# A third weight's products split into even and odd banks in every second unit of a fused FFT and max-out kernel

## The chip, the cores and the metric

The kernel runs on one core of a Trainium2 chip. Its engines work from queues of their own and meet through semaphores: TensorE (PE in the profile; its weight loads are PEld), VectorE (DVE), ScalarE (ACT), GpSimd (POOL) and SyncE (SP, which here only issues DMAs). Matmuls write to PSUM, which has eight banks of 512 float32 per partition; GpSimd is given SBUF operands only in this kernel. The metric is the device time of one execution in microseconds.

## The reference

```python
# x: (8, 3072, 256)
X = np.fft.fft(x, axis=1)
X = np.fft.fft(X, axis=2)
t = X.real.astype(np.float32).reshape(8 * 3072, 256)
# w1, w2, w3: (256, 768), w_out: (768, 256)
h = np.maximum(np.maximum(t @ w1, t @ w2), t @ w3)
out = (h @ w_out).astype(np.float32)
```

So there is a real part of a two-dimensional Fourier transform for each of 8 batches, and then a feed-forward layer of 24,576 tokens whose hidden value is the maximum over three products.

## The kernel before, in words

**The mathematics.** For each batch the transform over the sequence is made in two stages, and the transform over the 256 features is not made at all: it is multiplied into the weights beforehand. A batch leaves two tables per feature, an even part `tE` and an odd part `tO`, each 128 partitions by 1536 positions. Position k and position 3072 - k use the same two tables: one needs "even plus odd", the other "even minus odd". The kernel calls them plus and minus, and the hidden values `hp` and `hm`. Partition 0 of `tO` is an exception: it holds a part that keeps its sign.

The maximum of three products is written as w1's product plus max(0, product with w2 - w1, product with w3 - w1). `gE[i]` and `gO[i]` hold the even and odd halves of the two difference weights (i = 0 for w2, i = 1 for w3), and `gD[i]` is `gO[i]` times `dif`, which is 0 on partition 0 and -2 elsewhere: adding `gD` times `tO` turns plus into minus. w1's own part goes straight through w_out as `gw`.

**The units.** The main loop (from L685) runs over 8 batches, 3 blocks of 512 positions in each, and 6 column groups `jc` of 128 hidden features: 18 units a batch, 144 in all. A unit has

- `unit_plus` (L392): four 512-column matmuls, gE and gO into the bank `pse2` and gE and gO into the bank `pse3`;
- `unit_out` (L409): ScalarE's relu of `pse2` into `stmp` (L412), then VectorE's maximum of `pse3` and `stmp` into `hp` (L413);
- `unit_minus` (L402): two matmuls with gD that add to the same two banks, and `unit_out` again into `hm`. These are issued in the next unit's turn, by `finish`, which is called behind that unit's plus.

Behind this, each unit issues ten steps of layer 2 (`l2_some(10)`), which work on the hidden values of the block before: `l2_block` (L426) makes, for each of four slots of 128 positions, one 512-column matmul (L445) and twelve 256-column ones (L422) into a bank `po`, and for two slots together two more (L437) that ScalarE copies to `even`. VectorE adds the two into `ot` (L450). SP stores the plus half (L462); GpSimd stores the minus half, whose rows run backwards, with an indirect DMA, the scatter (L455), and a small memset behind it (L459).

**The transform of the next batch** is spread over the units by a plan written out by hand (`at`, `piece`, `late`, `ahead0`, `ahead`): `s` pieces (L336) multiply x into `tb`, `y` stores that to DRAM, `z` loads it back transposed as `yb`, `x0` and `c` put in a separate row, which GpSimd copies into `yb` (L374), and `k` pieces (L376) make 512 positions of `tE` or `tO`, copied by ScalarE (L383). In inner batches the `s` pieces stand in units 1 to 4, `z` in 7, `c` in 11 and the `k` pieces in 13 to 17. `fetch` (L650) makes GpSimd load x of a batch, in four parts, into one of two buffers; `turn` (L654) makes VectorE write a mirrored copy of it (L126, L127). Both have places in the plan: for batch b, fetches in units 9 to 12 and mirrors in units 14 to 17 of batch b - 2.

**What sets the order.** Every engine executes in the order in which the Python program issues: there is no scheduler. Waits come from tile dependencies and from pools. PSUM is divided as `ps_f` 2 banks (transform pieces, `pl`, some products of the preparation), `ps_l1` 2 each for `pse2` and `pse3`, and `ps_o` 2 for `po`.

**The start.** Before the loop, x of batch 0 is loaded and mirrored, angles are computed by VectorE (L255), tables by ScalarE (L260), the first halves of the weights are multiplied by the feature transform (L274, L286), and the first `k` pieces are made: `m.k(0, 0, dve)` (L590), whose copy is VectorE's, and `m.k(1, 0)` (L591). `angles(1024, NHALF + 1)` stands ahead of them (L587).

## Time and profile before

| | us |
|---|---|
| median of 3 runs | 418.67 (417.16 to 418.86) |
| the profiled execution | 418.88 |
| its span | 417.1 |
| PE busy | 397.2 (95%) |
| DVE busy | 293.2 (70%) |
| ACT busy | 251.7 (60%) |
| POOL busy | 151.1 (36%) |
| one inner batch | 47.15 |

The page's second part cuts the span in 40 slices: PE shows 9 in nearly all slices behind the start, DVE mostly between 5 and 8, POOL mostly between 1 and 6. An inner batch is a stretch such as 217.74 to 264.90, from one batch's first `hm` to the next's. Matmul records last longer than the distance between them, because they are pipelined: for the time that a matmul costs, read the distance between starts. The same holds, to a smaller degree, for VectorE's operations.

### The profile page before, as it was taken

The numbers are of one execution on the slowest core, as the hardware profiler recorded it, in microseconds if no ns is written. First come the engines' busy times: TensorE is split into PE (matmuls) and PEld (weight loads), VectorE is DVE, ScalarE is ACT, GpSimd is POOL, SyncE is SP. The second block draws the span as 40 slices with busy tenths as digits, with TensorE's granted clock in tenths as the row PEclk, the third lists the DMA queues.
The fourth block names the chain that finished last, engine by engine and source line by source line (L and its number), as shares of the span: only waits on it lengthen the run. The fifth ranks groups of instructions, "written<-read, shape, count | busy, mean of one in ns | idle before, by whom it ended". The sixth has DMA issues, their size and how long they took to land.

```text
span 417.1 us, 8143 instructions
## 1 busy us (share of the span) xinstructions
PE 397.2 (95%) x2741; PEld 249.1 (60%) x2790; DVE 293.2 (70%) x524; ACT 251.7 (60%) x474; POOL 151.1 (36%) x269
## 2 busy tenths in 40 slices
PE   7669899999999999999999999999999999999995
PEld 2235456666666666666666666656665666656664
DVE  7868656867785677857785676857785676667772
ACT  2547667665666657675567657675567656655550
POOL 7370123423622443323632443324532432333430
PEclk9989999999999999999999999999999999999998
DMA  8998246936952579236962569235962552222224
GB/s 123 193 179 129 65 120 159 175 93 159 199 139 68 122 186 186 81 89 151 203 148 60 133 174 193 85 88 125 223 149 60 139 159 65 78 61 63 83 75 127
DMA packets 66334, 53.27 MB, mean 128 GB/s; under 512 B 34649, under 2 KB 61890, under 8 KB 65094
## 3 DMA queue, kind: packets, MB, share of 16 engines
q0 software_dynamic: 23376, 26.27, 32.3%
q1 hardware_dynamic: 41748, 25.82, 23.7%
q10 hardware_dynamic: 1168, 0.65, 0.6%
q8 instruction: 22, 0.36, 0.4%
q14 instruction: 20, 0.16, 0.1%
HBM read 35.14 MB, written 31.69 MB: 160 GB/s over the span
## 4 chain that ended last, share of the span: by engine, by line
PE 84%; DVE 6%; ACT 3%; DMA 3%; issue 2%; POOL 1%; DVEq 0%; SPq 0%; ACTq 0%; POOLq 0%
PE po L422 28%; PE pse L398 15%; PE pse L406 13%; PE pse L399 12%; PE po L445 4%; PE ps L340 4%; PE pl L437 3%; PE ps L381 2%; DMA xt<-in_x_dram 2%; DVE hm L413 2%; ACT stmp L412 2%; DVE xt L126 1%; POOL xt L121 1%; DMA out_dram<-ot 1%; DVE ot L450 0%
## 5 line engine op out<-in xcount | busy, mean ns | idle before, releaser
L412 ACT ACTIVATE stmp<-pse 128x512 bf16<-128x512 f32 x288 | 169.9, 601 | 81.7 <-PE pse L399 61.0
L455 POOL DMA_INDIRECT out_dram<-ot,rows_m x92 | 103.8, 1128 | 238.4 <-DVE ot L450 209.4
L413 DVE TENSOR_TENSOR hp<-pse,stmp 128x512 bf16<-128x512 f32 x144 | 99.6, 691 | 105.0 <-PE pse L406 63.8
L398 PE MATMUL pse<-tE,gE 128*128 128x512 bf16 x287 | 109.4, 381 | 4.5 <-DVE tE L383 2.7
L413 DVE TENSOR_TENSOR hm<-pse,stmp 128x512 bf16<-128x512 f32 x144 | 99.0, 688 | 1.0 <-ACT stmp L412 0.9
L399 PE MATMUL pse<-tO,gO 128*128 128x512 bf16 x249 | 95.0, 382 | 0.1
L422 PE MATMUL po<-wout_bf,hp 128*128 128x256 bf16 x576 | 86.1, 273 | 0.0
L406 PE MATMUL pse<-tO,gD 128*128 128x512 bf16 x280 | 83.9, 379 | 0.5
L422 PE MATMUL po<-wout_bf,hm 128*128 128x256 bf16 x576 | 78.6, 273 | 0.0
L422 PEld LDWEIGHTS <-hp 128*128 128x128 bf16 x576 | 56.4, 98 | 26.1
L422 PEld LDWEIGHTS <-hm 128*128 128x128 bf16 x576 | 56.4, 98 | 16.3
L450 DVE TENSOR_TENSOR ot<-po,even 128x512 f32<-128x512 f32 x92 | 62.9, 683 | 0.2
L406 PEld LDWEIGHTS <-gD 128*128 128x128 bf16 x288 | 27.6, 98 | 32.0
L342 ACT CAST tb<-ps 128x512 bf16<-128x512 f32 x48 | 26.1, 588 | 28.4 <-PE ps L340 27.2
L399 PEld LDWEIGHTS <-gO 128*128 128x128 bf16 x288 | 28.2, 98 | 25.0 <-issue 4.1
L398 PEld LDWEIGHTS <-gE 128*128 128x128 bf16 x288 | 28.3, 98 | 22.5 <-issue 1.0
L445 PE MATMUL po<-gw,tO 128*128 128x512 bf16 x92 | 34.9, 379 | 0.0
L340 PE MATMUL ps<-xt,tabz 128*128 128x512 bf16 x96 | 25.1, 379 | 4.5 <-DVE xt L127 4.4
L441 ACT COPY even<-pl 128x512 f32<-128x512 f32 x46 | 27.0, 587 | 0.0
L383 ACT CAST tO<-ps 128x512 bf16<-128x512 f32 x24 | 14.1, 586 | 16.9 <-PE ps L381 9.3
L121 POOL DMA_DIRECT2D xt<-in_x_dram x36 | 23.4, 657 | 0.0
L126 DVE COPY xt<-xt 64x1524 bf16<-64x1524 bf16 (+4 forms) x32 | 19.1, 598 | 5.1 <-DMA xt<-in_x_dram 4.4
(134 smaller groups left out, 219.4 us busy)
## 6 DMA issues: line engine op xcount, KB each, us to landing
yb<-db SPq DMA_DIRECT2D x7, 833.0 KB
xt<-in_x_dram POOLq DMA_DIRECT2D x14, 384.0 KB
out_dram<-ot SPq DMA_DIRECT2D x56, 96.0 KB
out_dram<-ot SPq DMA_DIRECT2D x64, 64.0 KB
db<-tb SPq DMA_DIRECT2D x21, 192.0 KB
xt<-in_x_dram POOLq DMA_DIRECT2D x7, 400.0 KB
xt<-in_x_dram POOLq DMA_DIRECT2D x7, 368.0 KB
out_dram<-ot SPq DMA_DIRECT2D x64, 32.0 KB
```

Source lines behind the costliest of these rows:

```text
L121: return nc.gpsimd.dma_start(out=xt[b % 2][32 * h:32 * h + 32, lo:hi, :], in_=src)
L340: nc.tensor.matmul(ps1, tab_at[hh], self.x[:, 8 * k + hh:8 * k + 8:2, 0:128], start=(hh == 0), stop=(hh == 1))
L398: nc.tensor.matmul(pse[:, 0:n], gE[i][:, js], te, start=True, stop=False)
L399: nc.tensor.matmul(pse[:, 0:n], gO[i][:, js], to, start=False, stop=True)
L406: nc.tensor.matmul(pse, gD[i][:, js], to, start=False, stop=True, skip_group_check=True)
L412: nc.scalar.activation(out=stmp[:, 0:n], in_=pses[0][:, 0:n], func=AX.Relu)
L413: nc.vector.tensor_tensor(out=dst, in0=src3, in1=stmp[:, 0:n], op=ALU.max)
L422: nc.tensor.matmul(po, hcols(jc), wout_bf[:, jc * 256:(jc + 1) * 256], start=False, stop=(jc == NJC - 1), skip_group_check=True)
L441: nc.scalar.copy(out=even, in_=pl)
L445: nc.tensor.matmul(po, to[:, cp], gw[:, 256:768], start=True, stop=True)
L450: nc.vector.tensor_tensor(out=ot.rearrange("p (h c) -> p h c", h=2), in0=po.rearrange("p (h c) -> p h c", h=2), in1=lin.unsqueeze(1).to_br ...
L455: stored(nc.gpsimd.indirect_dma_start(out, bass.IndirectOffsetOnAxis(ap=rows_m[0:128 - lo, b * 12 + slot: b * 12 + slot + 1], axis=0), ot[ ...
```

## The change

From unit 7 of the whole run on, every odd unit is *split*. A split unit's third weight no longer goes through plus and minus in one bank. Instead `third(g)` makes the even product gE[1] times tE into one bank `e3` and gD[1] times tO into another, `d3`. ScalarE copies `d3` times -0.5, which is the odd part without its partition 0. VectorE copies `e3` and adds partition 0's part: the row `tO[0]`, spread to all partitions in `vb`, times a column of weights `wcol`. GpSimd adds and subtracts the two copies into `plus3` and `minus3`. The unit's own output is then one VectorE operation: the maximum of 0, `pse2` and `plus3`, and for minus the same with `minus3`. ScalarE has no relu in split units.

`third(g)` is issued in the turn of unit g - 2, behind the minus of unit g - 3 (for units 7 and 13, in the turn before their own). The row `tO[0]` is written to DRAM (`vds`) by SP and read back with a broadcast (`v`), both in the plan near the `k` pieces, whose order in `late` is changed. The column `wcol` is made once, in unit 5, with 24 one-column matmuls.

Other moves come with it. PSUM is divided anew: `ps_f` 3, `pse2` 2, one bank for `pse3` of even units (`ps_w3`), `ps_o` 2. The scatter is issued in the unit after its slot. A batch's minus of its last unit is carried into the next batch. x is fetched a batch earlier, in units 9 to 12 of batch b - 3, and mirrored in units 5, 7, 9 and 11 of batch b - 2. In the start, the tables for 512 to 1024 follow the second product, the last angles go to units 6 and 7 and their tables to units 8 and 9, and two warm-up matmuls are dropped. The middle positions' steps (`l2_mid`) are made in two goes.

```diff
-    ps_f = ctx.enter_context(tc.tile_pool(name="ps_f", bufs=2, space=bass.MemoryType.PSUM))
+    ps_f = ctx.enter_context(tc.tile_pool(name="ps_f", bufs=3, space=bass.MemoryType.PSUM))
...
+    def angle(part, c0=1024, c1=NHALF + 1):
+        cs = slice(c0, c1)
+        if part == 0:
+            scal(kvec[:, cs], kvec[:, cs], s_of, ALU.mult, phi, ALU.add)
+            scal(q[:, cs], kvec[:, cs], 1.0 / 3072.0, ALU.mult, ROUND, ALU.add)
+        else:
+            scal(q[:, cs], q[:, cs], -ROUND, ALU.add, -3072.0, ALU.mult)
+            nc.vector.tensor_tensor(out=kvec[:, cs], in0=kvec[:, cs], in1=q[:, cs], op=ALU.add)
...
+    def column():
+        psc = ps_f.tile([128, 512], FP32, name="psc", tag="ps")
+        for jc in range(NJC):
+            for k, (table, wt) in enumerate(((md, w3_bf), (nmd, w1_bf))):
+                for fc in range(2):
+                    nc.tensor.matmul(psc[:, jc:jc + 1],
+                                     wt[:, fc * DFF + jc * 128: fc * DFF + jc * 128 + 128],
+                                     table[fc][:, 128:129],
+                                     start=(k == 0 and fc == 0), stop=(k == 1 and fc == 1))
+        nc.scalar.copy(out=wcol, in_=psc[:, 0:NJC])
...
             evict(out=(self.tE, self.tO)[which][:, g * 512:(g + 1) * 512], in_=ps2)
+            if which and (self.b or g):
+                cs = slice(g * 512, (g + 1) * 512)
+                nc.sync.dma_start(out=vds[self.b % 2][:, cs], in_=self.tO[0:1, cs])
+
+        def v(self, g):
+            cs = slice(g * 512, (g + 1) * 512)
+            nc.sync.dma_start(out=self.vb[:, cs],
+                              in_=vds[self.b % 2][:, cs].to_broadcast([128, 512]))
...
-            stored(nc.gpsimd.indirect_dma_start(
...
-            nc.gpsimd.memset(mark, 0.0)
+            waiting.append((b * 12 + slot, lo, ot))
...
-    tables(512, 1024)
     for half in range(2):
         keep_product(product(1, half, 0, ps_s, "ps"), 1, half, 0, dve)
-    angles(1024, NHALF + 1)
-    warm_up(8)
+    tables(512, 1024)
+    warm_up(6)
...
+    ps_w3 = ctx.enter_context(tc.tile_pool(name="ps_w3", bufs=1, space=bass.MemoryType.PSUM))
+    s_pool = ctx.enter_context(tc.tile_pool(name="sums", bufs=3))
...
-            at(b - 2, (9, 10, 11, 12)[ch], lambda b=b, ch=ch: fetch(b, ch))
-            at(b - 2, (14, 15, 16, 17)[ch], lambda b=b, ch=ch: turn(b, ch))
+            at(b - 3, (9, 10, 11, 12)[ch], lambda b=b, ch=ch: fetch(b, ch))
+            at(b - 2, (5, 7, 9, 11)[ch], lambda b=b, ch=ch: turn(b, ch))
-    late = {13: ("kE0",), 14: ("kO0", "kE1"), 15: ("kO1",), 16: ("kE2",), 17: ("kO2", "end")}
+    late = {13: ("kO0",), 14: ("v0", "kE0", "kO1"), 15: ("v1", "kE1"), 16: ("kO2",),
+            17: ("v2", "kE2", "end")}
...
+    def is_split(g):
+        return g % 2 == 1 and 7 <= g < B * UNITS
...
+    def third(g):
+        js, te, to, vb, jc = operands(g)
+        e3 = ps_f.tile([128, TOKB], FP32, name="e3", tag="ps")
+        nc.tensor.matmul(e3, gE[1][:, js], te, start=True, stop=True)
+        d3 = ps_f.tile([128, TOKB], FP32, name="d3", tag="ps")
+        nc.tensor.matmul(d3, gD[1][:, js], to, start=True, stop=True)
+        even3, odd3 = (s_pool.tile([128, TOKB], FP32, name=n, tag=n) for n in ("even3", "odd3"))
+        nc.scalar.activation(out=odd3, in_=d3, func=AX.Copy, scale=-0.5)
+        nc.vector.scalar_tensor_tensor(out=even3, in0=vb, scalar=wcol[:, jc:jc + 1], in1=e3,
+                                       op0=ALU.mult, op1=ALU.add)
+        sums[g] = [s_pool.tile([128, TOKB], BF16, name=n, tag=n) for n in ("plus3", "minus3")]
+        for dst, op in zip(sums[g], (ALU.add, ALU.subtract)):
+            nc.gpsimd.tensor_tensor(out=dst, in0=even3, in1=odd3, op=op)
+
+    def begin(g, dst):
+        js, te, to, _, jc = operands(g)
+        if is_split(g):
+            pse2 = ps_l1.tile([128, TOKB], FP32, name="pse2", tag="pse2")
+            nc.tensor.matmul(pse2, gE[0][:, js], te, start=True, stop=False)
+            nc.tensor.matmul(pse2, gO[0][:, js], to, start=False, stop=True)
+            nc.vector.scalar_tensor_tensor(out=dst, in0=pse2, scalar=0.0, in1=sums[g][0],
+                                           op0=ALU.max, op1=ALU.max)
+            return (pse2,)
+        pses = unit_plus(te, to, jc, TOKB, *((ps_o, "po") if g % 2 else (ps_w3, "pse3")))
+        unit_out(pses, dst, TOKB)
+        return pses
+
+    def finish(g, pses, dst):
+        js, te, to, _, jc = operands(g)
+        unit_minus(pses, to, jc)
+        if is_split(g):
+            nc.vector.scalar_tensor_tensor(out=dst, in0=pses[0], scalar=0.0, in1=sums.pop(g)[1],
+                                           op0=ALU.max, op1=ALU.max)
+        else:
+            unit_out(pses, dst, TOKB)
...
+        pses = begin(g, hp[:, jc, :])
+        if prev is not None:
+            finish(*prev)
+        prev = (g, pses, hm[:, jc, ::-1] if last else hm[:, jc, :])
+        for lead in (1, 2):
+            if is_split(g + lead) and (lead == 1) == (g + lead in (7, 13)):
+                third(g + lead)
+        scatter()
+        l2_some(10)
```

More of the change, by code (lines that the diff above doesn't have):

```diff
@@ L531, with scatter @@
     l2_queue = []
+    waiting = []
+    def scatter():
+        while waiting:
+            at_row, lo, ot = waiting.pop(0)
+            stored(nc.gpsimd.indirect_dma_start(
+                out, bass.IndirectOffsetOnAxis(
+                    ap=rows_m[0:128 - lo, at_row: at_row + 1], axis=0),
+                ot[lo:128, 256:512], None), "scattered", ("scattered", "direct"))
+            nc.gpsimd.memset(mark, 0.0)
     def l2_some(n):
@@ L642, in piece @@
             mm.c()
+        elif what[0] == "v":
+            mm.v(int(what[1]))
         elif what[0] == "k":
@@ new lines @@
+        pses = begin(g, hp[:, jc, :])
[7 more added lines that the diff above has]
+        l2_some(10)
+        if b == B - 1 and u in (1, 3):
+            if u == 1:
+                middle = l2_mid()
+            next(middle, None)
+        for fn in plan.get((b, u), ()):
+            fn()
```

99 lines of the change are left out of this document (43 added, 56 removed).

## The prediction, made before the changed kernel had run

> **What bounds the kernel now.** I read the page's busy times, then the table by stage of five inner batches, then the timeline of one unit, then the chain of waits and the groups.
>
> ```profile
> PE 397.2 (95%) x2741; PEld 249.1 (60%) x2790; DVE 293.2 (70%) x524; ACT 251.7 (60%) x474; POOL 151.1 (36%) x269
> ```
> ```profile
> 170.60:217.74 47.14, 46.82 (x329) 29.76 (x334) 33.73 (x57) 30.25 (x57) 17.83 (x31) 1.00 0.61 137
> 217.74:264.90 47.16, 46.84 (x329) 29.80 (x334) 33.73 (x57) 30.25 (x57) 17.82 (x31) 1.00 0.60 137
> 264.90:312.06 47.16, 46.84 (x329) 29.81 (x334) 33.73 (x57) 30.21 (x57) 17.83 (x31) 1.00 0.60 137
> ```
>
> The columns are length, then busy time of PE, weight loads, DVE, ACT, POOL, then the granted clock, the DMA share and GB/s. Every inner batch takes 47.15 us, and PE is idle for 0.32 of it. Busy PE alone proves little, so the starts matter:
>
> ```profile
> 202.48 0.38 PE L398 MATMUL pse<-tE,gE 128*128 128x512 bf16 x1
> ...
> 202.70 0.38 PE L399 MATMUL pse<-tO,gO 128*128 128x512 bf16 x1
> ...
> 202.91 0.38 PE L398 MATMUL pse<-tE,gE 128*128 128x512 bf16 x1
> ...
> 203.13 0.38 PE L399 MATMUL pse<-tO,gO 128*128 128x512 bf16 x1
> ...
> 203.34 0.59 PE L406 MATMUL pse<-tO,gD 128*128 128x512 bf16 x2
> ```
>
> Start to start is 0.215 us for 512 columns. A batch holds 108 of these in its units, 24 more in L445 and L340, some 160 half-size ones, and 36 table pieces: at those spacings about 47 us. So PE streams without gaps: a matmul taken out is worth 0.215 us, as long as nothing else becomes late. The chain of waits agrees (PE 84% of the span). The other engines' groups:
>
> ```profile
> L412 ACT ACTIVATE stmp<-pse 128x512 bf16<-128x512 f32 x288 | 169.9, 601 | 81.7 <-PE pse L399 61.0
> L455 POOL DMA_INDIRECT out_dram<-ot,rows_m x92 | 103.8, 1128 | 238.4 <-DVE ot L450 209.4
> L413 DVE TENSOR_TENSOR hp<-pse,stmp 128x512 bf16<-128x512 f32 x144 | 99.6, 691 | 105.0 <-PE pse L406 63.8
> ```
>
> **The change, part by part.** *Matmuls.* From unit 7 on every odd unit is split: 69 of 144. Each goes from six to five 512-column matmuls: 69 x 0.215 = **-14.9 us**, the only large term. The new column adds 24 one-column matmuls; the nearest rows, the 8-column ones of the middle rows, start 0.026 apart: **+0.6** once.
>
> *ScalarE.* A split unit trades two relus (2 x 0.60) for one copy of the odd product (0.59 by the other 512-wide copies): 30.25 - 9 x 0.61 = 24.8 us of some 45.2 per batch. Hidden; without that cover it is still a saving.
>
> *VectorE.* It keeps two operations per split unit and gains the even sum. A TENSOR_TENSOR takes 0.69, and back to back starts come 0.605 apart; a scale read from a tensor costs up to 0.06 more (the angle scaling with two of them takes 0.544, the same width with constants 0.427). So 0.67 to 0.75 each, nine per batch: 33.7 + 6.4 = 40.1 of 45.2 us. It fits on the mean, but not everywhere. In units 5 to 12 there is no transform work, and a pair of units costs PE only 21 x 0.215 = 4.54 us (11 full-size in the units, 10 in layer 2). VectorE there needs four outputs (2.42), one even sum (0.67), 1.33 output evictions (0.81) and, where the mirrors now stand, one mirror pair (0.70 by its spacing): 4.6. Lag after four pairs: about 0.3 us. The slack, from an hp's end to the third weight's minus matmul that needs its bank, is 1.5 us (202.05 to 203.55), so: nothing.
>
> *GpSimd.* Two additions of 128x512 f32 per split unit have no row. The nearest are:
>
> ```profile
> L708 POOL COPY tEr<-tE 128x512 bf16<-128x512 bf16 x1 | 0.6, 617 | 0.0
> ```
> ```profile
> 30.20 0.20 POOL L604 TENSOR_TENSOR adj<-low 128x1 f32<-128x1 f32 x1
> ...
> 30.48 0.39 POOL L605 TENSOR_TENSOR rows_f<-rows_f,adj 128x96 f32<-128x96 f32 x1
> ```
>
> One input of full width takes 0.62: the lower end. The 96-column addition scaled in proportion gives 2.06: the upper end. The line through the two additions, 0.20 + 2.0 ns a column, gives 1.2, which I take since it is the same operation. Then POOL carries 17.8 + 18 x 1.2 = 39.4 us of 45.2. The scatter now stands a unit later, so it rarely waits; it delays the additions behind it by 0.96 to 1.18 each. In units 9 to 12 four fetches (0.66 each) come too, and then the copy into yb, which waits for the batch's yb load; before, that wait was 3.0 us over three batches. Behind it stand a scatter, a fetch and unit 15's additions, and for those VectorE waits. Unit 15 is wanted two units after its products, with about 1.2 us to spare. Taken as nothing, at most 1 us a batch.
>
> *PSUM.* The even product holds one of three ps_f banks until VectorE has done hp, hm and the even sum, some 2.7 us into the unit; in units 3 and 15, where pl follows, PE wants that bank for a transform piece at 2.4. About 0.3 us twice a batch; ScalarE's release of the other bank is earlier. I take 0.45 a batch in seven batches, **+3.1**; bounds 0 and 1.7 (the second rival's).
>
> *SP queue.* Three row writes and three broadcasts per batch. The write waits for tO's copy, the broadcast for the write to land, and output stores queue behind both; six ot buffers at 3.8 us a slot cover over 20 us. The first broadcast is wanted by unit 17's VectorE sum, three units (7.5 us) after unit 13; eviction about 1, two landings at 2.5 (a stored tb chunk is read back that soon in the prologue): 6. Nothing, with 1.5 us to spare.
>
> *Fetch and mirrors.* x arrives a batch earlier, so mirrors stop waiting for it (4.4 us of VectorE waits in all, none ending PE's idle time in inner batches): nothing. The stores of the same bytes move, none is added.
>
> *Start.* Before, the first unit waits for tE, and that for angles:
>
> ```profile
> 24.57 0.69 DVE L26 TENSOR_TENSOR kvec<-kvec,q 128x513 f32<-128x513 f32 x1
> ...
> 25.18 0.68 DVE L383 CAST tE<-ps 128x512 bf16<-128x512 f32 x1
> ...
> 25.91 0.58 PE L398 MATMUL pse<-tE,gE 128*128 128x512 bf16 x1 [2.71 <-DVE tE L383]
> ```
>
> The angles (22.9 to 25.2) leave this place, so tE can be out at 23.7; ScalarE's second table now ends about 22.9, with c and tO after it, so unit 0 starts near 23.9: **-2.0**. Bounds: 0, if the second half of the weights (requested at 22.65) holds unit 1; -3.7, if the half-rate stretch after the gap (granted clock 0.50 from 26 to 29) goes too. The angles return in units 6 and 7, ahead of mirrors for which PE already waits 0.97 at 49.1: **+1.5**, between 0 and 2.3, their length.
>
> *Last block.* Its final minus needs no relu (0.60), but PE runs on there without a gap: nothing.
>
> Sum: -14.9 + 0.6 + 3.1 - 2.0 + 1.5 = **-11.7**. The profiled execution took 418.88 (span 417.1 and 1.8 around it), 0.2 above the median 418.67; from the median that is **407.0**.
>
> **A rule against it.** Mirror copies and POOL's work already touch each other: the scatter takes 0.96 alone and 1.14 to 1.18 beside a mirror, while the mirror keeps its 0.55. The Trainium skill, SBUF — State Buffer, section Who interferes with whom, says that the port pair VectorE shares with GpSimd is locked for a whole instruction, so that one of the two fully blocks. By that rule the sum would be rival 2's; the trace so far shows only the 0.2 us.
>
> **The rivals.**
> 1. *All covers hold.* No bank wait, no clock dip, and the angles fit: -14.9 + 0.6 - 3.7 = 400.7. For it: VectorE's 13.4 us idle per batch. Against: the 4.54 us pairs.
> 2. *Mirrors stand behind additions.* If a copy has to wait for a running addition, POOL adds in about half of units 5 to 12, so each mirror pair loses 0.6 to 1.2, say 0.65, four times a batch: 2.6, with the 0.3 above 2.9 against 1.5 of slack and some 0.3 for catching up late: 1.7 us lost a batch in six batches. With the other terms: 418.7 - 16.3 + 1.5 + 10 = 413.9; with half of it, 409. I put it at 410 to 417.
> 3. *GpSimd becomes the bound: slower than before.* Its place is the pair of additions. The point is where 17.83 + 18 t = 47.15: t = 1.63 us. At the proportional 2.06 a batch takes 54.9, so seven cost 54 more: about 470; at 1.75, 434. For it: POOL's rows are rough and small. Against: the line gives 1.2.
> 4. *The first broadcast comes late*, and VectorE with its queue (outputs, evictions) stops at each batch's start. For it: the 833 KB yb load took some 9 us to land. Each us beyond the 1.5 to spare costs 7, so the gain of 11.7 is gone from 1.7 us late. Two landings of 4.5 us come 2.5 late: 407 + 17 = 424.
>
> **How the numbers follow.** Forecast 0.43 (403 to 410), rival 1 0.22, rival 2 0.16, rival 3 0.12, rival 4 0.07. The range 400.5 to 416 holds nearly all of the first three, 0.80; the likeliest alone is 403 to 410. Half a per cent, 2.1 us, is about what a measurement of this kernel can tell from no change. Faster: 0.43 + 0.22 + 0.14 + 0.02 = 0.81; same: 0.02 + 0.03 = 0.05; slower: 0.12 + 0.02 = 0.14.
>
> **What would show it.** Inner batches near 45.7 us with POOL near 39 and VectorE near 40 busy; GpSimd additions near 1.2 us; unit 0 near 24 us; few PE waits, on ps_f by VectorE. Additions above 1.6 us, mirrors longer than 0.6, or VectorE waiting on vb at unit 17 would prove me wrong.

## The result and the profile after

The changed kernel took 488.5 us (median of 4 runs, 487.06 to 489.14) against 418.37 us for the kernel before (417.16 to 418.86): a ratio of 1.168, with an interval of 1.164 to 1.171. The forecast was 407.0 in a range of 400.5 to 416. It is wrong by 81.5 us and on the wrong side.

The matmuls did go: the weight loads, one for each matmul, fall from 2790 to 2743, which is 69 less for the split units, 2 less for the warm-up and 24 more for the column. (Of the kernel before, some 50 matmul records are missing, so PE's own counts hardly differ.) What they freed was lost several times over. The first lines of the page of the kernel after, and the first line of its chain of waits:

```profile
PE 407.4 (84%) x2743; PEld 247.0 (51%) x2743; DVE 375.7 (77%) x593; ACT 217.8 (45%) x406; POOL 327.7 (67%) x407
...
PE 52%; DVE 17%; issue 11%; DMA 9%; POOL 7%; ACT 2%; SPq 0%; DVEq 0%; POOLq 0%
```

PE held 95% of the span and 84% of the chain before; now it holds 84% and 52%, and no other engine is full either. That is the mark of engines waiting for each other in turn, not of a new bound. The table by stage of the kernel after shows an inner batch and then the one batch (the seventh) that transforms a next batch but mirrors no x. Columns: the stretch, its length, busy time of PE, weight loads, DVE, ACT and POOL, the granted clock, the DMA share and GB/s.

```profile
270.13:326.40 56.27, 48.18 (x325) 29.59 (x325) 45.79 (x65) 25.86 (x48) 41.01 (x49) 0.97 0.53 121
382.50:430.59 48.09, 46.51 (x324) 28.97 (x324) 37.07 (x57) 25.86 (x48) 37.18 (x45) 1.00 0.39 110
```

The two stretches have the same matmuls but one, the same ScalarE work and the same additions. The eight VectorE instructions more are the four mirrors of x (two copies each): they make VectorE 8.7 us busier, though the same eight copies take 3 us where nothing stands beside them (4 x 0.74), and the batch 8.2 us longer.

To see where the 69 us of span went, I count each batch from VectorE's first `hp` to the next batch's first, in the timelines of all profiles (us; batches numbered from 0; the kernels below the first two are the experiments of the next part):

| kernel | first hp | batch 0 | mean of 1 to 5 | batch 6 | last 17 steps | span |
|---|---|---|---|---|---|---|
| before | 27.9 | 50.9 | 47.2 | 47.0 | 41.95 | 417.1 |
| after | 26.3 | 73.0 | 56.4 | 48.1 | 43.6 | 486.4 |
| mirrors on ScalarE | | 71.5 | 51.8 | 48.1 | 43.6 | 460.9 |
| the same with VectorE filler | | 70.0 | 51.8 | 48.1 | 43.6 | 460.0 |
| minus first | | 72.5 | 53.8 | 46.1 | 40.2 | 467.4 |
| before, with x's moves | | 58.4 | 47.7 | 47.2 | 41.95 | 426.5 |
| mirrors ahead of even sums | | 64.3 | 51.2 | 48.2 | 43.6 | 452.0 |
| both | | 64.7 | 49.3 | 46.1 | 40.2 | 437.3 |
| both, x fetched later | | 61.9 | 49.5 | 46.1 | 40.2 | 433.5 |
| the same, angles early | 26.6 | 60.1 | 49.5 | 46.1 | 40.2 | 434.3 |
| last two batches only | 27.5 | 49.9 | 47.6 | 48.3 | 40.2 | 417.1 |
| units 3 to 11 too | 28.0 | 51.6 | 50.2 | 48.3 | 40.2 | 432.7 |
| last two, late angles | 27.7 | 51.8 | 47.6 | 48.3 | 40.2 | 419.4 |
| from unit 11 of batch 6 | 28.1 | 49.9 | 47.5 | 47.9 | 40.2 | 416.7 |

In the table, "last 17 steps" is the way from the last batch's first `hp` to its eighteenth. For the change: -1.6 at the start, +22.1 in batch 0, 5 x 9.2 = +46.0 in batches 1 to 5, +1.1 and +1.7 in the last two: 69.3. So three things have to be explained: batches with mirrors, batch 0, and a small loss even in the batches where nothing stands in the way.

The groups of the kernel after that name them (busy us and mean ns of one, then the idle time of the engine just before them and what ended it):

```profile
L752 POOL TENSOR_TENSOR plus<-even,odd 128x512 bf16<-128x512 f32 x69 | 90.9, 1317 | 117.8 <-DVE even L748 117.8
...
L759 PE MATMUL pse<-tE,gE 128*128 128x512 bf16 x69 | 26.4, 383 | 47.6 <-DVE hm L773 47.1
...
L748 DVE SCALAR_TENSOR_TENSOR even<-vb,wcol,e 128x512 f32<-128x512 bf16 x69 | 51.0, 739 | 6.1 <-DMA vb<-vd 6.1
```

PE's largest wait, 47.1 us before the first matmul of a split unit (L759), is for VectorE's `hm` (L773): the minus output of the split unit before, two units back. That wait did not exist before, and the prediction has no line for it.

**A mirror beside an addition.** The timeline of the kernel after, inside an inner batch (start, length, engine, line):

```profile
243.44 1.26 POOL L752 TENSOR_TENSOR plus<-even,odd 128x512 bf16<-128x512 f32 x1 [4.10 <-DVE even L748]
...
243.93 1.19 DVE L128 COPY xt<-xt 64x1524 bf16<-64x1524 bf16 x1
...
244.67 1.57 POOL L752 TENSOR_TENSOR minus<-even,odd 128x512 bf16<-128x512 f32 x1
245.04 1.25 DVE L129 COPY xt<-xt 64x12 bf16<-64x12 bf16 x1
...
246.32 0.69 DVE L444 TENSOR_TENSOR hp<-pse,stmp 128x512 bf16<-128x512 f32 x1
246.93 0.68 DVE L773 SCALAR_TENSOR_TENSOR hm<-pse,minus 128x512 bf16<-128x512 f32 x1
```

The large copy starts 0.49 us into the first addition and ends at 245.12, 0.42 behind the addition's end at 244.70: its own length is 0.55. The second addition, which starts while that copy runs, takes 1.57 in place of 1.26. The small copy moves 12 elements a partition and takes 1.25: it ends at 246.29, just behind the second addition at 246.24. Each waits out the other. Over the run, the small copy of the kernel after, then of the kernel before (minimum/median/maximum ns):

```profile
L129 DVE COPY xt<-xt x32: 166/1191/1257, 9.1 to 363.4; 64x12 bf16<-64x12 bf16 x21, 64x13 bf16<-64x13 bf16 x7, 64x16 bf16<-64x16 bf16 x2, 64x8 bf16<-64x8 bf16 x1
```
```profile
L127 DVE COPY xt<-xt x32: 166/184/507, 8.4 to 313.3; 64x12 bf16<-64x12 bf16 x21, 64x13 bf16<-64x13 bf16 x7, 64x16 bf16<-64x16 bf16 x2, 64x8 bf16<-64x8 bf16 x1
```

This is what the Trainium skill, SBUF — State Buffer, section Who interferes with whom, says of VectorE's copies in their two-port modes and of GpSimd: whoever issues first has the shared port pair for the whole instruction. The trace agrees, down to a 12-element copy that lasts as long as an addition.

A copy can also stand out two additions. That happens once in each of batches 1 to 5, in unit 7, where the first addition has begun just before the copy (235.47) and the second follows it at once (to 237.94):

```profile
235.67 2.69 DVE L128 COPY xt<-xt 64x1524 bf16<-64x1524 bf16 x1
...
239.85 0.58 PE L759 MATMUL pse<-tE,gE 128*128 128x512 bf16 x1 [2.91 <-DVE hm L773]
```

The copy takes 2.69 in place of 0.55, and PE's wait behind it, 2.9, is the longest that it has for `hm`.

**A split unit without mirrors.** The timeline of the kernel after in batch 6:

```profile
407.96 0.38 PE L437 MATMUL pse<-tO,gD 128*128 128x512 bf16 x1
...
408.36 0.69 DVE L444 TENSOR_TENSOR hp<-pse,stmp 128x512 bf16<-128x512 f32 x1 [0.23 <-PE pse L437]
408.97 0.68 DVE L773 SCALAR_TENSOR_TENSOR hm<-pse,minus 128x512 bf16<-128x512 f32 x1
...
409.70 0.38 PE L759 MATMUL pse<-tE,gE 128*128 128x512 bf16 x1 [0.27 <-DVE hm L773]
```

The minus matmul (L437) ends the stream that the split unit's `hm` needs, but VectorE's queue has the next unit's `hp` first. So `hm` ends at 409.65, and PE, which needs the bank of `pse2` for the split unit after, stands 0.27 us. In the kernel before that bank came free with ScalarE's relu. A pair of units goes from L759 at 404.72 to 409.70: 4.98 us, against 2 x 2.385 = 4.77 for a pair of the kernel before. Where no wait is left, in the minus-first kernel below, the split pair takes 4.55 (from L759 at 425.25 to 429.80). So the pair loses 0.43; the wait shows less, since a matmul's record lasts longer than the distance to the next. The 1.5 us of slack in the prediction do not exist on this path: it is short before any mirror comes.

**The clock.** PE's wait of 2.9 us comes once in each of batches 1 to 5 (2.91 to 2.94). With four of the five the clock granted falls to 0.50, for some 3.4 us (6.8 in batch 3); with the fifth, 2.93 at 352.84, it stays at 1.00. Four lines of the table by stage of the kernel after (columns as above, the granted clock third from the end): two stretches behind the wait that ends at 239.85, then the way from the end of such a wait to the second L759 behind it, in a batch with the low clock and in the one without:

```profile
240.00:243.50 3.50, 3.50 (x11) 1.39 (x10) 2.24 (x4) 1.44 (x3) 0.06 (x1) 0.50 0.51 196
246.50:250.00 3.50, 3.33 (x25) 2.17 (x23) 3.26 (x6) 1.19 (x2) 2.10 (x4) 1.00 0.75 118
...
183.76:197.52 13.76, 11.10 (x59) 6.33 (x59) 12.55 (x17) 4.64 (x8) 8.59 (x9) 0.88 0.69 154
352.84:366.61 13.77, 9.43 (x60) 5.75 (x60) 12.56 (x17) 4.64 (x8) 7.32 (x7) 1.00 0.28 91
```

At 0.50 PE is busy throughout and does 11 matmuls where a stretch of the same length at 1.00 holds 25 (of mixed sizes). But the two longer stretches, one with the low clock and one without, take the same 13.8 us: VectorE is busy for 12.55 us of them, and PE at full clock only waits longer for it at the L759 in between (2.49 in place of 0.82). The batches say so too: 56.1 without, 56.1 to 56.7 with. So the low clock, which takes part in bringing the mean of the span from 0.993 to 0.963, is a consequence of the waits, and by this comparison it explains at most 0.6 us of a batch. The comparison is not a pure one: the batch without the low clock has no x to fetch either.

**Batch 0.** The angles, which the change moved beside the first additions, meet the same lock. The timeline of the kernel after:

```profile
48.18 1.38 DVE L196 TENSOR_SCALAR q<-kvec 128x513 f32<-128x513 f32 x1
...
54.89 1.63 DVE L264 TENSOR_TENSOR kvec<-kvec,q 128x513 f32<-128x513 f32 x1
...
57.27 1.03 PE L363 MATMUL ps<-xt,tabz 128*128 128x512 bf16 x2 [5.42 <-DVE xt L129]
...
85.40 0.61 PE L404 MATMUL ps<-to_tab,yb 98*128 98x96 bf16 x6 [7.66 <-POOL yb L397]
```

Before, these two operations of the angles (L196, L264) took 0.43 and 0.69. The mirror of the next batch stands behind them, and PE waits 5.42 us for it. The other wait, 7.66, ends a chain: the copy into `yb` on GpSimd (85.07) stood behind a split unit's additions (from 80.30), those behind VectorE's even sum (79.39), and that behind a broadcast of `vb` that came 4.26 us late. Behind both waits the clock granted is 0.50 for some microseconds (57 to 60 and 84 to 87).

### The profile page after: what moved, and what is told of

Its sections match the earlier page's. It is cut to its first block, busy times and chain, and to the rows that moved or that the text cites. A ratio compares the mean times of both kernels' runs of the same rounds, so it can differ in the third digit from the quotient of the medians.

```text
span 486.4 us, 8355 instructions
## 1 busy us (share of the span) xinstructions
PE 407.4 (84%) x2743; PEld 247.0 (51%) x2743; DVE 375.7 (77%) x593; ACT 217.8 (45%) x406; POOL 327.7 (67%) x407
## 3 DMA queue, kind: packets, MB, share of 16 engines
q0 software_dynamic: 23376, 26.27, 27.5%
## 4 chain that ended last, share of the span: by engine, by line
PE 52%; DVE 17%; issue 11%; DMA 9%; POOL 7%; ACT 2%; SPq 0%; DVEq 0%; POOLq 0%
PE po L453 14%; PE pse L437 8%; DVE hm L773 6%; PE pse L759 5%; PE pse L429 4%; PE pse L430 4%; DVE even L748 3%; PE d L745 3%; PE e L743 3%; PE pse L760 3%; DMA vb<-vd 3%; DVE hp L444 3%; PE ps L363 3%; POOL minus L752 2%; DVE ot L481 2%
## 5 line engine op out<-in xcount | busy, mean ns | idle before, releaser
L752 POOL TENSOR_TENSOR plus<-even,odd 128x512 bf16<-128x512 f32 x69 | 90.9, 1317 | 117.8 <-DVE even L748 117.8
L443 ACT ACTIVATE stmp<-pse 128x512 bf16<-128x512 f32 x150 | 90.0, 601 | 144.8 <-PE pse L437 113.8
L752 POOL TENSOR_TENSOR minus<-even,odd 128x512 bf16<-128x512 f32 x69 | 89.5, 1297 | 0.0
L444 DVE TENSOR_TENSOR hp<-pse,stmp 128x512 bf16<-128x512 f32 x75 | 51.8, 690 | 37.8 <-ACT stmp L443 27.2
L761 DVE SCALAR_TENSOR_TENSOR hp<-pse,plus 128x512 bf16<-128x512 f32 x69 | 47.7, 691 | 41.9 <-PE pse L760 38.7
L437 PE MATMUL pse<-tO,gD 128*128 128x512 bf16 x219 | 72.7, 389 | 0.0
L759 PE MATMUL pse<-tE,gE 128*128 128x512 bf16 x69 | 26.4, 383 | 47.6 <-DVE hm L773 47.1
L429 PE MATMUL pse<-tE,gE 128*128 128x512 bf16 x150 | 58.4, 389 | 0.4 <-DVE hm L444 0.3
L430 PE MATMUL pse<-tO,gO 128*128 128x512 bf16 x150 | 58.2, 388 | 0.3 <-ACT tO L406 0.3
L444 DVE TENSOR_TENSOR hm<-pse,stmp 128x512 bf16<-128x512 f32 x75 | 51.8, 691 | 6.6 <-ACT stmp L443 2.0
L748 DVE SCALAR_TENSOR_TENSOR even<-vb,wcol,e 128x512 f32<-128x512 bf16 x69 | 51.0, 739 | 6.1 <-DMA vb<-vd 6.1
L773 DVE SCALAR_TENSOR_TENSOR hm<-pse,minus 128x512 bf16<-128x512 f32 x69 | 47.0, 681 | 0.0
L747 ACT ACTIVATE odd<-d 128x512 f32<-128x512 f32 x69 | 41.2, 597 | 11.3 <-PE d L745 5.1
```

The lines of the kernel that those rows point to most:

```text
L429: nc.tensor.matmul(pse[:, 0:n], gE[i][:, js], te, start=True, stop=False)
L430: nc.tensor.matmul(pse[:, 0:n], gO[i][:, js], to, start=False, stop=True)
L437: nc.tensor.matmul(pse, gD[i][:, js], to, start=False, stop=True, skip_group_check=True)
L443: nc.scalar.activation(out=stmp[:, 0:n], in_=pses[0][:, 0:n], func=AX.Relu)
L444: nc.vector.tensor_tensor(out=dst, in0=src3, in1=stmp[:, 0:n], op=ALU.max)
L748: nc.vector.scalar_tensor_tensor(out=even3, in0=vb, scalar=wcol[:, jc:jc + 1], in1=e3, op0=ALU.mult, op1=ALU.add)
```

## The experiments

Four readings stand against each other. The *lock*: GpSimd's additions and VectorE's copies hold each other up, and the delay reaches PE. The *load*: VectorE simply has too much to do. The *order* of `hp` and `hm`, which leaves no slack. And *x's moves*: x a batch earlier, in the DMA queues and on SP.

**Mirrors on ScalarE.** In the changed kernel:

```diff
     def turn(b, ch):
-        mirror(b, *CHUNKS[ch])
+        s0, s1 = CHUNKS[ch]
+        t = xt[b % 2]
+        nc.scalar.copy(out=t[64:128, s0:s1, 1:128], in_=t[0:64, s0:s1, 255:128:-1])
+        nc.scalar.copy(out=t[64:128, s0:s1, 0], in_=t[0:64, s0:s1, 128])
```

> The changed kernel with the mirror copies inside the loop made by ScalarE instead of VectorE. Theory A (port): VectorE's mirror copies stand behind GpSimd's additions, 0.75 us of copies becoming up to 2.4; without them on VectorE every inner batch falls from 56.4 to the 48.1 that the last full batch, which has no mirrors, already shows, and part of batch 0's extra 22 goes: 488.5 - 5 x 8.3 - about 8 = 439. Theory B (load): VectorE simply has too much to do in units 5 to 12; it expects the same here. Theory C (GpSimd's queue: the additions come late because scatters and fetches stand ahead of them): VectorE would still wait for plus and minus, and the time stays above 470.

Measured: 460.75 us, 1.101 [1.088, 1.114]. Inner batches fell from 56.4 to 51.8, half of what they had lost, and batch 0 hardly moved. The copies are out of the lock's reach, but a mirror takes 1.70 us on ScalarE (1.46 and 0.24) where it takes 0.74 on a free VectorE, and the relus stand behind it: I take that for the reason why the 439 us that were expected did not come.

**The same, with filler on VectorE.** In `turn`, behind the ScalarE copies:

```diff
+        nc.vector.memset(vm[:, 0:512], 0.0)
+        nc.vector.memset(vm[:, 0:128], 0.0)
```

> As the run with mirrors on ScalarE, but VectorE gets two memsets of float32 (512 and 128 columns, results unused) in the mirrors' places, about 0.55 and 0.2 us, as long as the undisturbed mirror copies, with nothing read from SBUF. Theory A (port): only the plain 0.75 us counts, and VectorE's order lets at most that through to PE, four times a batch: 439 plus 0 to 18. Theory B (load): the time stays at 480 or more.

Measured: 461.86 us, 1.104 [1.097, 1.111]; inner batches 51.8, the same to 0.01 us. The filler gives VectorE its load back, about as long as a mirror (0.66 against 0.74), and inner batches do not change: load alone does not make the 4.6 us between 56.4 and 51.8. (Since ScalarE's copies may leave VectorE room in this kernel, the run with the mirrors ahead is the stronger test.) The large memset of that kernel also shows that additions do not hold it up: 24 of the 28 stand beside one, and all take the same time (minimum/median/maximum ns):

```profile
L698 DVE MEMSET vm<- x28: 485/485/485, 38.3 to 337.3; 128x512 f32 x28
```

**Minus first.** When the previous unit is split, its minus matmul and `hm` go ahead of the next unit's plus:

```diff
+        first_minus = prev is not None and is_split(prev[0])
+        if first_minus:
+            finish(*prev)
         pses = begin(g, hp[:, jc, :])
-        if prev is not None:
+        if prev is not None and not first_minus:
             finish(*prev)
```

> The changed kernel, but behind a split unit its minus is issued ahead of the next unit's plus, on TensorE and VectorE, instead of behind it. Theory A with the bank's release as its second part: a split unit's pse2 bank is now freed by VectorE's hm, which stands behind the next unit's hp; 0.27 us of PE wait per pair without mirrors (4.985 against 4.72) goes, and beside mirrors up to 0.65 of slack appears at each of the four: 488.5 - 8 x 9 x 0.27 = 469 to 475 with part of the mirrors' cost hidden as well, down to 460. If the order of hm and hp does not matter: 488.

Measured: 468.95 us, 1.121 [1.113, 1.128]. Batch 6 falls from 48.1 to 46.1 and the last batch's steps from 43.6 to 40.2: both are now below the kernel before (47.0 and 41.95). The timeline of this kernel, in batch 6:

```profile
398.05 0.68 DVE L773 SCALAR_TENSOR_TENSOR hm<-pse,minus 128x512 bf16<-128x512 f32 x1
398.65 0.68 DVE L444 TENSOR_TENSOR hp<-pse,stmp 128x512 bf16<-128x512 f32 x1
...
399.09 0.38 PE L759 MATMUL pse<-tE,gE 128*128 128x512 bf16 x1
```

`hm` now ends before the bank is wanted, and L759 shows no wait; the time is what was expected (469 to 475). The order was a cause: this is the whole loss of the undisturbed batches, and the split by itself does pay. Over nine split units 1.7 us are gained in the last batch, 0.19 each, of the 0.215 that the matmul is worth.

**The kernel before, with x's moves alone.**

```diff
-        at(0, (13, 14, 15, 16)[ch], lambda ch=ch: fetch(2, ch))
-        at(0, (17, 18, 19, 20)[ch], lambda ch=ch: turn(2, ch))
+        at(0, (1, 2, 3, 4)[ch], lambda ch=ch: fetch(2, ch))
+        at(0, (9, 10, 11, 12)[ch], lambda ch=ch: turn(2, ch))
...
-            at(b - 2, (9, 10, 11, 12)[ch], lambda b=b, ch=ch: fetch(b, ch))
-            at(b - 2, (14, 15, 16, 17)[ch], lambda b=b, ch=ch: turn(b, ch))
+            at(b - 3, (9, 10, 11, 12)[ch], lambda b=b, ch=ch: fetch(b, ch))
+            at(b - 2, (5, 7, 9, 11)[ch], lambda b=b, ch=ch: turn(b, ch))
```

> The kernel before, with one part of the change alone: x fetched a batch earlier and mirrored in units 5, 7, 9 and 11; no unit is split. Theories A and B: nothing is lost, 418 within 2 (VectorE has room there without even sums, and GpSimd has no additions). If the new places of the fetches and mirrors cost time by themselves (theory D): 430 or more.

Measured: 429.72 us, 1.027 [1.017, 1.037]. Expected was 418, or 430 if the moves cost time by themselves, and it is the second: without any split unit, the moves alone cost 7.5 us in batch 0 and 0.5 in each inner batch (from one profile; the two runs took 428.3 and 431.1). The waits of PE in this kernel say how (us in total, times, the longest):

```profile
PE ps L381 <- DMA yb<-db: 5.3, 2, 5.1
```

Two batches' fetches now fall into batch 0, and the load of `yb` comes 5.1 us late. That the one makes the other was not tested here; the later fetch, below, bears on it. So x's moves are a part of batch 0, and hardly one of the inner batches.

**Mirrors ahead of the even sums.** The copies are issued just ahead of `third`, so that the additions of the split unit before are over and the next have not begun. In inner batches the units stay the same; in batch 0, batch 2's mirrors go from units 9 to 12 to units 9, 11, 13 and 15:

```diff
-        at(0, (4, 5, 6, 7)[ch], lambda ch=ch: turn(1, ch))
+        before_third(0, (4, 5, 6, 7)[ch], lambda ch=ch: turn(1, ch))
...
-        at(0, (9, 10, 11, 12)[ch], lambda ch=ch: turn(2, ch))
+        before_third(0, (9, 11, 13, 15)[ch], lambda ch=ch: turn(2, ch))
...
-            at(b - 2, (5, 7, 9, 11)[ch], lambda b=b, ch=ch: turn(b, ch))
+            before_third(b - 2, (5, 7, 9, 11)[ch], lambda b=b, ch=ch: turn(b, ch))
...
+        for fn in early.get((b, u), ()):
+            fn()
         for lead in (1, 2):
```

> The changed kernel with each mirror pair still on VectorE and in the same odd units, but issued just ahead of the even sum instead of behind it (in batch 0, batch 2's mirrors in units 9, 11, 13 and 15). GpSimd's additions for a unit start only when that sum is done, so at this place most of the former unit's additions have ended. Theory A (port): the small copy of 12 elements goes back from about 1.2 to 0.18 us and the large one to 0.55; inner batches fall from 56.4 to 48.1 plus at most 4 x 0.75, and the total to 440 to 455. If the copies are slow for another reason (their data, VectorE's load, the units they stand in), nothing changes: 488.

Measured: 454.68 us, 1.089 [1.082, 1.096]. In inner batches the same engine does the same copies in the same units, some operations earlier, and they fall from 56.4 to 51.2; batch 0, where units changed too, from 73.0 to 64.3. The small copy of this kernel:

```profile
L129 DVE COPY xt<-xt x32: 164/182/506, 8.1 to 328.1; 64x12 bf16<-64x12 bf16 x21, 64x13 bf16<-64x13 bf16 x7, 64x16 bf16<-64x16 bf16 x2, 64x8 bf16<-64x8 bf16 x1
```

Its median is 182 ns again. This is the cleanest test of the lock against the load, and the lock holds: 5.2 of the 9.2 us in an inner batch.

**Both, then x fetched later, then the angles early.** Three steps, each on top of the one before: minus first with the mirrors ahead; then

```diff
-            at(b - 3, (9, 10, 11, 12)[ch], lambda b=b, ch=ch: fetch(b, ch))
+            at(b - 2, (0, 1, 2, 3)[ch], lambda b=b, ch=ch: fetch(b, ch))
```

and then

```diff
-                    (6, lambda: angle(0)), (7, lambda: angle(1)), (8, lambda: table(1)),
+                    (2, lambda: angle(0)), (3, lambda: angle(1)), (8, lambda: table(1)),
```

> As the run before, with the split unit's minus ahead of the next unit's plus as well. If the port and the bank's release are the two costs of inner batches, both go: inner batches 46.1 to 47, the total 425 to 437, what is left being batch 0 (about 20 above before). If the two are one cost seen twice: no better than the run before by more than 5.

> As the run before, with x fetched in units 0 to 3 of batch b - 2 instead of units 9 to 12 of batch b - 3. In batch 0 the fetch of batch 3 then no longer runs beside the load of yb, for which TensorE waited 5.1 us in the kernel before with early x. If that load causes batch 0's wait for the copy into yb (7 to 9 us): 6 to 9 us less than the run before. If GpSimd's queue causes it: within 2 of it.

> As the run before, with the last angles in units 2 and 3 instead of 6 and 7. Theory A: their four VectorE operations read SBUF beside GpSimd's first additions and take 5.0 us there instead of 2.3; ahead of the first split unit they take 2.3 again and TensorE's waits for mirrors in batch 0 (1.8 and 5.4) shrink: 3 to 6 us less than the run before. If these waits come from x arriving late: the same as the run before.

Measured: 439.83 us (1.054 [1.048, 1.060]), 436.81 (1.046 [1.037, 1.056]) and 435.68 (1.044 [1.039, 1.049]). The two cures add up: another 1.9 us from each inner batch, to 49.3, though 46.1 to 47 were expected. The later fetch, which takes one of the two fetches out of batch 0, gave 2.8 us there and nothing elsewhere; 6 to 9 were expected if the late load made the wait. With the angles early, their four operations are back at 0.54, 0.43, 0.42 and 0.70, so the lock on them is gone, and batch 0 is 1.8 us shorter. But it also begins 2.1 later, and the two kernels' times overlap (435.3 to 438.3 and 435.3 to 436.1): a gain from this move is not shown, where 3 to 6 were expected. What stays over the kernel before is 9.2 us in batch 0 and 2.3 in each inner batch. The timeline of the last of the three kernels, over one pair of units with a mirror and what comes behind it:

```profile
200.00 0.69 DVE L766 SCALAR_TENSOR_TENSOR hp<-pse,plus 128x512 bf16<-128x512 f32 x1 [1.34 <-PE pse L765]
200.78 0.69 DVE L444 TENSOR_TENSOR hm<-pse,stmp 128x512 bf16<-128x512 f32 x1
201.50 0.62 DVE L128 COPY xt<-xt 64x1651 bf16<-64x1651 bf16 x1
202.04 0.17 DVE L129 COPY xt<-xt 64x13 bf16<-64x13 bf16 x1
202.25 0.75 DVE L753 SCALAR_TENSOR_TENSOR even<-vb,wcol,e 128x512 f32<-128x512 bf16 x1
202.92 0.68 DVE L481 TENSOR_TENSOR ot<-po,even 128x512 f32<-128x512 f32 x1
203.52 0.68 DVE L778 SCALAR_TENSOR_TENSOR hm<-pse,minus 128x512 bf16<-128x512 f32 x1
204.12 0.68 DVE L444 TENSOR_TENSOR hp<-pse,stmp 128x512 bf16<-128x512 f32 x1
204.95 0.69 DVE L766 SCALAR_TENSOR_TENSOR hp<-pse,plus 128x512 bf16<-128x512 f32 x1 [0.15 <-PE pse L765]
...
207.12 2.55 POOL L563 DMA_INDIRECT out_dram<-ot,rows_m  x1
...
209.73 1.27 POOL L757 TENSOR_TENSOR plus<-even,odd 128x512 bf16<-128x512 f32 x1
...
211.04 0.69 DVE L766 SCALAR_TENSOR_TENSOR hp<-pse,plus 128x512 bf16<-128x512 f32 x1 [1.11 <-POOL plus L757]
...
214.52 0.39 PE L476 MATMUL po<-gw,tO 128*128 128x512 bf16 x1 [0.85 <-DVE ot L481]
```

In the first pair no copy is locked, and VectorE is all but back to back: 4.95 us, where PE's matmuls are 4.55. So here, once the lock is gone, the load counts after all: the even sum and the mirror make VectorE the bound. The next pair, from 204.95 to 211.04, loses more, and not by load. One scatter of each batch takes 2.55 us, in the kernel before too (seven of 92; the group's mean of 1.13 hides them). Here it stands ahead of a unit's additions, VectorE is idle for 1.11 us until `plus` is there, its sum out of the bank `po` is late by that, and PE stands 0.85 for the bank. PE's waits list that one in five batches, 4.2 us in all. From the `hp` of unit 5 to that of unit 11 this kernel takes 16.18 us (200.00 to 216.18) against 14.31 before (187.05 to 201.36): 1.9 of the 2.3. How this share divides between VectorE's load and GpSimd's queue is read from the trace, not tested by a run of its own.

**Only where nothing stands beside.** The kernel before, with its own order of x, angles and tables; split units only in batches 6 and 7 (17 of them), minus first, and `pse3`'s idle buffer for the even product. The change's later scatter, its order of `k` pieces and the minus that is carried into the next batch stay in these kernels:

```diff
+    def is_split(g):
+        return g % 2 == 1 and 6 * UNITS + 3 <= g < B * UNITS
...
+        e3 = ps_l1.tile([128, TOKB], FP32, name="e3", tag="pse3")
```

Then units 3, 5, 7, 9 and 11 of the batches before too, and, on the first of the two, the change's late angles (units 6 and 7, tables in 8 and 9) alone.

> The kernel before, with its own order of x, angles and tables and its own two banks for ps_f, and with the split units only where no copy of x stands beside them: 17 odd units of batches 6 and 7, the second minus matmul's output taken ahead of the next unit's first. The even product takes the idle buffer of pse3, the odd one ps_f. Theory (the split pays by itself, about 0.11 us a split unit, and everything lost came from VectorE's copies beside the additions and from x and the angles in batch 0): batch 6 falls from 47.0 to 46.1 us and the last 17 units from 41.95 to 40.2, as in the minus-first run, so 418.4 - 0.95 - 1.7 = 415.7. Rival (the gain seen there came from the third ps_f buffer or from another place of the change): batch 6 stays at 47.0 or above, the whole at 418 or above.

> The same, and in batches 1 to 5 units 3, 5, 7, 9 and 11 split too (from 5 on in batch 1), so that the additions end before the copies of x in units 14 to 17: 24 more split units, 41 in all. Theory: 24 x 0.11 = 2.6 us more, batches 1 to 5 at 46.6 each, 413.1 in all. Rival (the batches lose by the GpSimd copies of yb and x0u and by ps_f's two buffers, not by the copies of x): batches 1 to 5 above 47.2 each, the whole at 416 or above.

> As the last-two-batches run, with the change's start alone added: the first tables after the second pair of products, the angles in units 6 and 7 and the tables in units 8 and 9, all without additions beside them. If the angles cost nothing when no addition stands beside them, unit 0 starts 1.6 us earlier and the time is 1.6 us below that run (414.1 if it takes 415.7); with the 1.5 us that the prediction gave to the angles the two are equal.

Measured: 419.11 us (1.0025 [0.9998, 1.0053]), 433.22 (1.035 [1.032, 1.037]) and 419.22 (1.0028 [1.0004, 1.0052]), where 415.7, 413.1 and 414.1 or 415.7 were expected. In all three the last 17 steps take 40.2, as the theory had it, and in the first and the third most batches without split units take what they took before (47.1 to 47.3), so the later scatter and the order of pieces cost nothing by themselves. Batch 6 does not fall to 46.1 but rises to 48.3, and the inner batches of the second kernel take 50.2. Where split units begin, one unit is 1.9 us longer: unit 1 of the second kernel takes 5.26 where it took 3.36. PE's waits of the first kernel over batch 6:

```profile
PE e L742 <- DVE hm L444: 1.2, 1, 1.2
```

The first even product waits for a bank that an unsplit unit still holds (1.2), and its two matmuls (0.43) come ahead of their unit. In the second kernel a later unit, 14, is as much longer, 5.0 to 5.3 in place of 3.12, and that is another matter:

```profile
221.68 0.62 DVE L128 COPY xt<-xt 64x1651 bf16<-64x1651 bf16 x1 [3.10 <-DMA xt<-in_x_dram]
```

VectorE stands at the first mirror until x has come, 3.0 to 3.2 us in each of five batches, and then PE for `hm` (1.6 to 1.9). GpSimd issues the fetches behind the additions: the first one 30.7 us into that batch (210.78), where the kernel before issues it after 26.6 (199.80). Together the two units are some 3.9 us longer; the batch lost 3.05, so the other units won some 0.85, 0.17 for each of the five that are split. My expectation had no price for either. The run with late angles equals the one without, as the 1.5 us of the prediction's angles would have it, but not for that reason: unit 0 did not start earlier (first `hp` 27.7 against 27.5). In this profile the clock granted was 0.50 from 19.5 to 23 us, while the last products ran; in the changed kernel's it was back at 1.00 from 21. With batch 0 between 49.9 and 51.6 in profiles of the same plan, one profile can't divide the rest.

**One boundary, elsewhere.** The first of these kernels, with the split begun at unit 11 of batch 6 and the first even product in `ps_f`:

```diff
+        pool3, tag3 = (ps_l1, "pse3") if is_split(g - 2) else (ps_f, "ps")
+        e3 = pool3.tile([128, TOKB], FP32, name="e3", tag=tag3)
```

> The last-two-batches run with the split begun at unit 11 of batch 6 instead of unit 3 (13 split units), and with the even product of the first split unit in ps_f instead of in pse3's buffer, which there is not yet idle. Theory (its batch 6 took 48.3 us because the first even product stood behind the minus half two units back): that wait of 1.2 us and the 1.9 us at units 1 and 2 go, batch 6 falls to 46.3 and the last 17 units stay at 40.2: 418.4 - 0.75 - 1.7 = 416.0, and 417.9 where the load of yb again comes 1.9 us late in one batch. Rival (a boundary between unsplit and split units costs by the order of the matmuls, wherever the product lies): batch 6 stays near 48 and the time at 419.

Measured: 419.0 us, 1.0037 [1.0013, 1.0060]. The wait on `hm` is gone, another stands in its place: unit 9 takes 3.66 in place of 2.38, two matmuls (0.43) and a wait for a bank of `ps_f`, which the odd product now holds.

```profile
340.66 0.38 PE L468 MATMUL pl<-gw,tE 128*128 128x256 bf16 x2 [0.69 <-ACT odd L747]
```

So the rival stands: where split units begin, more is lost than a matmul, wherever the product lies. The three kernels with split units in the last batches alone also scatter more, 416.6 to 422.9 us where the kernel before lies between 416.8 and 419.6. In the profiles of all three it is batch 4, which has no split unit, that is longer: 49.1, 49.3 and 48.2 against 47.2. There the copy behind the `yb` load starts 14.0 us after the load's issue in the first kernel (241.24 to 255.27), 9.2 in the kernel before. Why that load is slower there stays open. No version here beats the kernel before.

## Why the prediction was wrong

*VectorE*, "The slack, from an hp's end to the third weight's minus matmul that needs its bank, is 1.5 us (202.05 to 203.55), so: nothing": this is the step that failed first. It takes the slack of `pse3`'s bank in an unsplit unit. The split unit moves the release of `pse2`'s bank from ScalarE's relu to VectorE's `hm`, which is queued behind the next unit's `hp`. The slack on that path is not 1.5 but less than nothing: a pair with no mirror near takes 4.98 us where 4.55 is enough, and the minus-first run gave 2.0 us of batch 6 back. So VectorE's delays reach PE: 47.1 us of waits before L759 in the whole run.

*Fetch and mirrors*, "nothing": the second failed step, and the large one. It looked only at what the mirrors wait for, not at what stands beside them in their new units. A mirror pair cost VectorE 2.2 us in place of 0.74 (8.7 over four pairs), four times a batch; putting the same copies ahead of the additions returned 5.2 us of the 9.2 that an inner batch had lost.

*A rule against it* and rival 2 named this mechanism, and gave it 1.7 us a batch and a chance of 0.16. The mechanism was right and its size wrong twice. It charged 0.65 a mirror pair where 1.4 came, since each of the two copies can stand out an addition and the large one both, and it set 1.5 us of slack against it that is not there. The row that I let speak against the rule, a scatter slowed by 0.2 us, was of an indirect DMA and not of an addition: the nearest row, but of another kind. Rival 2's sum of 413.9 also leaves out the +3.1 of the forecast for `ps_f`; with it, it is 417.0.

The lag of "about 0.3 us" after four pairs was too small as well: without any lock, three pairs with mirrors lost 1.9 us. A part of that belongs to the step on *GpSimd*, where a scatter delays the additions behind it "by 0.96 to 1.18": it left out the one scatter a batch of 2.55, behind which VectorE then stood 1.11.

*Angles*, +1.5 with a bound of 2.3, "their length": the bound took their length from a place without additions. Beside them they took up to 1.38 and 1.63 instead of 0.43 and 0.69, and held back a mirror for which PE waited 5.42. What moving them is worth in the time is not shown. Of batch 0, 8.7 us came back with the mirrors ahead of the even sums, some of them in other units, and 2.8 with one fetch moved out; x's moves alone had cost the unsplit kernel 7.5, and for them the step on the fetches had nothing either. The last 9.2 us of batch 0 stay unexplained in part: PE still waits 5.0 there for the copy into `yb`.

*SP queue*, "Nothing, with 1.5 us to spare", and rival 4: right in the inner batches, where VectorE never waited for `vb`. In batch 0 the even sum waited twice, 1.8 and 4.3 us.

*GpSimd*, 1.2 us an addition from a line through two small rows: it took 1.26 where no copy stood beside it and 1.30 to 1.32 on the mean, and the point from which GpSimd would be the bound, 1.63, was not reached. Rival 3 ended on the right side for a reason that was not the one.

*PSUM*, +3.1 for `ps_f`: not seen. PE's waits list one of 1.0 us there in the whole run. *Start*, -2.0: the first `hp` came 1.6 us earlier, and over all profiles with this start and three banks of `ps_f` at 24.5 to 26.6, against 27.3 to 28.1 with the old one. *Matmuls*, -14.9: real, but only in the batches that nothing disturbs, 0.19 of the 0.215 us a unit in the last batch, and only with the minus first.

The sign that the prediction asked for was the right one: "mirrors longer than 0.6" among those that "would prove me wrong". The common form of the large copy took 1.26 on the mean, against 0.56 before.

## What to carry to other kernels

When work moves to GpSimd, list what VectorE does in the same microseconds, by kind of operation. In these traces copies, scalings and a sum of two SBUF operands stood still behind an addition, a whole one however small the copy and once a batch two, while memsets and operations with an operand in PSUM did not. Put the first kind into the window where GpSimd is idle, by order of issue, before counting any cover. List too what else stands in GpSimd's queue, by its longest row and not by its mean. And when an output's last reader changes engine, follow the bank that it frees to the matmul that wants it, in the order of that engine's queue: a slack read off the old reader is no slack of the new one.

## What the runs showed that I had not expected

- A copy of 12 elements a partition went from 0.18 to 1.25 us beside an addition, a large one from 0.55 to 2.69 beside two; the addition beside a copy went from 1.26 to 1.57.
- VectorE's maxima with one operand in PSUM kept their 0.69 us, and memsets their 485 ns, beside the same additions.
- With four of five waits of 2.9 us PE's clock was granted at 0.50 for 3.4 us or twice that, with the fifth not; a stretch behind them took 13.8 us with the low clock and without, since PE would have waited for VectorE anyway.
- One scatter a batch takes 2.55 us where the others take about 1. In the kernel before GpSimd was idle behind it; here additions stand there and come late.
- Where split units begin, one unit is 1.3 to 1.9 us longer, 0.43 of it for two matmuls that come forward.
